# Attention and a Gelu feed-forward on one core: both stages rebuilt around 128x1536 units, with x kept in SBUF

## The chip, the cores and the metric

The kernel runs on one core of one Trainium2 chip. In the views, PE is TensorE's matmuls and PEld its weight loads, ACT is ScalarE, DVE is VectorE, POOL is GpSimd and SP is SyncE; PSUM is the memory that matmuls write to, and a bank is the part of it that a tile of 512 float32 columns takes in these kernels. The granted clock (PEclk) is the share of TensorE's full clock that the throttle allowed. The metric is the device time of one execution in microseconds; medians of several executions are quoted with their extremes. Every ratio uses runs of a kernel and of the kernel before on the same chip in the same session.

An execution is marked "slow" when it is over 1.5% longer than the fastest one of the same kernel, and verdicts use the fast ones alone.

## The reference, cut to what matters

```python
B, C, Hh, Ww = (4, 128, 384, 32)                 # q: (4, 12288, 128), kv: (4, 384, 32, 128)
kv_pool = kv.reshape(B, H // 4, 4, W // 4, 4, C).mean(axis=(2, 4))
k = v = kv_pool.reshape(B, -1, C) @ w_sr         # 768 keys of 128 per batch
s = (q @ k.T) / sqrt(C)
a = softmax(s)
x = (a @ v).reshape(B * S, C)                    # 49152 rows
h = x @ w_in                                     # 128 -> 2048
out = (h * sigmoid(1.702 * h)) @ w_out           # 2048 -> 128
```

So 49152 x 768 exponentials, 49152 x 2048 Gelus, and four large matrix products. No batch attends to another. Both kernels leave out the subtraction of the maximum, which the sizes of the inputs allow.

## The kernel before: the parts that the change touches

It has three stages, one after the other, each with pools of its own. In the first, all keys and values are made. Every 128 rows of kv are one 32 KB load, and a matmul with a small averaging matrix pools them:

```python
for b in range(B):
    poolT_ps = ppsum.tile([128, J], F32)
    for hh in range(Hp):                                   # 96 per batch
        kvt = kvload.tile([128, 128], BF)
        nc.gpsimd.dma_start(out=kvt, in_=kv_flat[b, hh * 128:(hh + 1) * 128, :])
        nc.tensor.matmul(poolT_ps[:, hh * Wp:(hh + 1) * Wp], kvt, M_sb, start=True, stop=True)
    # ... keys, and values by transposing the keys ...
```

The second is attention in steps of 256 rows. All six key chunks of a step lie in one PSUM tile of three banks, of which there is one (`spsum`, `bufs=1`):

```python
sT_ps = spsum.tile([128, JC, TQ * 128], F32)
for jc in range(JC):
    nc.tensor.matmul(sT_ps[:, jc, :], kT[:, jc * 128:(jc + 1) * 128], qT, start=True, stop=True)
a_all = apool.tile([128, JC, TQ * 128], BF)
nc.scalar.activation(a_all, sT_ps, AF.Exp, scale=scale)
# ... sums by a ones column, reciprocal of one row, broadcast, values, product ...
nc.sync.dma_start(out=xT_dram[...], in_=xT)                # x goes to memory
```

The third reads x back, group by group of 512 rows, and runs 16 Gelus of 512 columns on each:

```python
for fc in range(FCH):
    hT_ps = hpsum.tile([128, G * 128], F32)                # one bank, two buffers
    nc.tensor.matmul(hT_ps, w_in_sb[:, fc * 128:(fc + 1) * 128], xT, start=True, stop=True)
    nc.scalar.activation(g_sb[:, fc, :], hT_ps, AF.Gelu_apprx_sigmoid)
# ... 16 accumulating matmuls, then four transposes, copies and stores of 64 KB ...
```

The softmax here doesn't subtract the row's maximum and nothing guards it: scores larger than these inputs give would overflow.

## Time and profile before

| stage | from, us | to, us | length, us | what limits it |
|---|---|---|---|---|
| kv | 0 | 288 | 288 | 384 small loads, issued one by one |
| attention | 288 | 1037 | 749 | a loop of waits through one PSUM buffer |
| feed-forward | 1037 | 1886 | 849 | ACT, by its busy time |
| end | 1886 | 1892 | 6 | last copies and store |

The median is 1892.09 us (1891.73 to 1893.77). On the page, the first line of section 1 gives each engine's busy time, its share of the span and its number of instructions. Section 2 cuts the span into 40 slices of equal length; each digit is a busy share in tenths.

```profile
PE 1395.2 (74%) x7643; PEld 702.0 (37%) x7712; DVE 628.8 (33%) x1273; ACT 1110.2 (59%) x1738; POOL 507.3 (27%) x978
...
PE   1222226666666666666665999999999999999998
...
ACT  0000003333333333333333999999999999999998
...
DMA  5555552222222222222221111111111111111111
```

The reader is to see the three stages as three plateaus, and that no row is full in the first two. An average such as "PE 74%" describes none of them. The prediction below reads each stage from its own waits.

### The profile page before, as it was taken

The page shows a single profiled execution, that of the slowest core. Times are in us where ns is not written, and L with a number is a line of the kernel's source. Part 1 is how long each engine was busy: PE and PEld are TensorE (multiplying, and loading weights), DVE is VectorE, ACT ScalarE, POOL GpSimd, SP SyncE. Part 2 cuts the span into 40 slices and gives each one's busy share as a digit, 9 for nine tenths or more (in the row PEclk, how much of TensorE's full clock was granted, in tenths as well). Part 3 has the DMA queues.
Part 4 walks back from the last instruction along what each step waited for, and adds up shares of the span by engine and source line. Part 5 has one row for each costly group of instructions (what it writes and reads, how often), then busy time and mean ns, then how long its engine had stood idle before and what let it go on. Part 6 is the DMA issues. An engine that isn't in the chain of part 4 may idle for free.

```text
span 1891.9 us, 22738 instructions
## 1 busy us (share of the span) xinstructions
PE 1395.2 (74%) x7643; PEld 702.0 (37%) x7712; DVE 628.8 (33%) x1273; ACT 1110.2 (59%) x1738; POOL 507.3 (27%) x978
## 2 busy tenths in 40 slices
PE   1222226666666666666665999999999999999998
PEld 0111114444444444444443333333333333333333
DVE  0000005666666666666665121211212112112121
ACT  0000003333333333333333999999999999999998
POOL 6777774433443443434432000000000000000000
PEclk9999999999999999999999999999999999999999
DMA  5555552222222222222221111111111111111111
GB/s 54 47 49 47 46 47 32 34 37 35 34 36 35 35 35 33 34 37 35 34 37 34 37 48 42 46 47 45 46 45 45 48 42 48 45 45 48 42 45 40
DMA packets 209829, 78.12 MB, mean 41 GB/s; under 512 B 123568, under 2 KB 209584, under 8 KB 209712
## 3 DMA queue, kind: packets, MB, share of 16 engines
q0 software_dynamic: 112944, 26.30, 15.2%
q1 hardware_dynamic: 96768, 50.37, 9.4%
q8 instruction: 60, 0.98, 0.2%
q14 instruction: 57, 0.47, 0.1%
HBM read 65.08 MB, written 37.75 MB: 54 GB/s over the span
## 4 chain that ended last, share of the span: by engine, by line
PE 51%; ACT 30%; DMA 8%; issue 7%; POOL 3%; DVE 1%; ACTq 0%; POOLq 0%
ACT g_sb L141 16%; PE hT_ps L139 16%; ACT a_all L107 14%; PE oT_ps L144 12%; PE ss_ps L110 8%; PE avT_ps L118 7%; DMA kvt<-in_kv_dram 7%; PE sT_ps L104 7%; POOL kvt L66 2%; PE o_ps L150 1%; DMA qt<-in_q_dram 1%; PE poolT_ps L67 1%; DVE rs L113 0%; POOL rs_bc L115 0%; ACTq L107 0%
## 5 line engine op out<-in xcount | busy, mean ns | idle before, releaser
L141 ACT ACTIVATE g_sb<-hT_ps 128x512 bf16<-128x512 f32 x1536 | 822.8, 597 | 22.6 <-PE hT_ps L139 22.0
L139 PE MATMUL hT_ps<-xT,w_in_sb 128*128 128x512 bf16 x1535 | 579.2, 377 | 35.0 <-ACT g_sb L141 29.6
L107 ACT ACTIVATE a_all<-sT_ps 128x1536 bf16<-128x1536 f32 x192 | 278.4, 1450 | 469.2 <-PE sT_ps L104 451.2
L144 PE MATMUL oT_ps<-g_sb,w_out_sb 128*128 128x512 bf16 x1468 | 550.0, 378 | 0.3 <-ACT g_sb L141 0.2
L113 DVE RECIPROCAL rs<-ss_ps 1x256 f32<-1x256 f32 x192 | 335.2, 1746 | 178.2 <-PE ss_ps L110 178.2
L147 DVE CAST oT<-oT_ps 128x512 bf16<-128x512 f32 x96 | 66.4, 692 | 634.7 <-PE oT_ps L144 634.7
L110 PE MATMUL ss_ps<-a_all,ones_col 128*1 128x256 bf16 x1152 | 158.6, 274 | 147.1 <-ACT a_all L107 147.1
L144 PEld LDWEIGHTS <-w_out_sb 128*128 128x128 bf16 x1536 | 147.3, 96 | 313.3 <-issue 278.3
L67 PE MATMUL poolT_ps<-M_sb,kvt 128*128 128x8 bf16 x384 | 72.0, 189 | 202.5 <-DMA kvt<-in_kv_dram 201.4
L66 POOL DMA_DIRECT2D kvt<-in_kv_dram x384 | 203.1, 533 | 65.0 <-PE poolT_ps L67 35.9
L139 PEld LDWEIGHTS <-w_in_sb 128*128 128x128 bf16 x1536 | 147.3, 96 | 187.9 <-issue 59.6
L115 POOL PARTITION_BROADCAST rs_bc<-rs x192 | 104.1, 543 | 420.7 <-DVE qT L101 391.5
L98 POOL DMA_DIRECT2D qt<-in_q_dram x384 | 207.1, 541 | 35.2 <-PE qT_ps L100 17.3
L110 PEld LDWEIGHTS <-ones_col 128*1 128x1 bf16 x1152 | 94.7, 83 | 199.9 <-issue 174.5
L70 ACT CAST poolT<-poolT_ps 128x768 bf16<-128x768 f32 x4 | 3.2, 798 | 274.2 <-PE poolT_ps L67 274.2
L118 PE MATMUL avT_ps<-a_all,v_all 128*128 128x256 bf16 x1152 | 161.2, 277 | 0.0
L104 PE MATMUL sT_ps<-qT,kT_all 128*128 128x256 bf16 x1152 | 159.8, 276 | 0.6 <-DVE qT L101 0.6
L100 PE MATMUL qT_ps<-ident,qt 128*128 128x128 bf16 x384 | 67.2, 218 | 99.0 <-DVE qT L101 90.3
L67 PEld LDWEIGHTS <-kvt 128*128 128x128 bf16 x384 | 40.5, 105 | 235.3 <-DMA kvt<-in_kv_dram 233.1
L104 PEld LDWEIGHTS <-kT_all 128*128 128x128 bf16 x1152 | 114.0, 99 | 15.5 <-issue 1.1
L118 PEld LDWEIGHTS <-v_all 128*128 128x128 bf16 x1152 | 97.6, 98 | 53.1 <-issue 43.7
L152 DVE CAST o_sb<-o_ps 128x128 f32<-128x128 bf16 x384 | 101.0, 289 | 49.1 <-PE o_ps L150 38.4
(28 smaller groups left out, 304.2 us busy)
## 6 DMA issues: line engine op xcount, KB each, us to landing
out_dram<-o_sb SPq DMA_DIRECT2D x384, 64.0 KB, 1.6
kvt<-in_kv_dram POOLq DMA_DIRECT2D x384, 32.0 KB, 2.1
qt<-in_q_dram POOLq DMA_DIRECT2D x384, 32.0 KB, 2.2
xT_scratch<-xT SPq DMA_DIRECT2D x192, 64.0 KB, 1.7
xT<-xT_scratch SPq DMA_DIRECT2D x96, 128.0 KB, 2.0
w_in_sb<-in_moe_w_in_dram POOLq DMA_DIRECT2D x1, 512.0 KB, 5.3
w_out_sb<-in_moe_w_out_dram POOLq DMA_DIRECT2D x1, 512.0 KB, 7.5
w_sr_sb<-in_w_sr_dram POOLq DMA_DIRECT2D x1, 32.0 KB, 2.2
```

Source lines behind the costliest of these rows:

```text
L66: nc.gpsimd.dma_start(out=kvt, in_=kv_flat[b, hh * 128:(hh + 1) * 128, :])
L67: nc.tensor.matmul(poolT_ps[:, hh * Wp:(hh + 1) * Wp], kvt, M_sb, start=True, stop=True)
L98: nc.gpsimd.dma_start(out=qt, in_=q[b, t * 128:(t + 1) * 128, :])
L104: nc.tensor.matmul(sT_ps[:, jc, :], kT[:, jc * 128:(jc + 1) * 128], qT, start=True, stop=True)
L107: nc.scalar.activation(a_all, sT_ps, AF.Exp, scale=scale)
L110: nc.tensor.matmul(ss_ps, ones_col, a_all[:, jc, :], start=(jc == 0), stop=(jc == JC - 1))
L113: nc.vector.reciprocal(rs, ss_ps)
L115: nc.gpsimd.partition_broadcast(rs_bc, rs)
L118: nc.tensor.matmul(avT_ps, v_all[:, b, jc, :], a_all[:, jc, :], start=(jc == 0), stop=(jc == JC - 1))
L139: nc.tensor.matmul(hT_ps, w_in_sb[:, fc * 128:(fc + 1) * 128], xT, start=True, stop=True)
L141: nc.scalar.activation(g_sb[:, fc, :], hT_ps, AF.Gelu_apprx_sigmoid)
L144: nc.tensor.matmul(oT_ps, w_out_sb[:, fc, :], g_sb[:, fc, :], start=(fc == 0), stop=(fc == FCH - 1))
```

## The change

The intent is to have ACT work without a pause from the first exponential to the last Gelu. Attention runs first for all batches, then the feed-forward for all rows, in one stream of 704 "units", each being three matmuls into a three-bank PSUM tile and one activation of 128x1536. There are two such tiles. PE fills unit n+2 and then drains an older unit: in attention the one ten units back, so that sums and reciprocals are ready when the values are. x never leaves SBUF. The diff, cut to its core:

```diff
-    xT_dram = nc.dram_tensor("xT_scratch", (B * NT // G, C, G * 128), BF, kind="Internal").ap()
+    q_bf = nc.dram_tensor("q_bf", (B * N, C), BF, kind="Internal").ap()
+    big = ctx.enter_context(tc.tile_pool(name="big", bufs=2, space=bass.MemoryType.PSUM))
+    ring = ctx.enter_context(tc.tile_pool(name="ring", bufs=2, space=bass.MemoryType.PSUM))
+    ctx.enter_context(tc.manual_schedule(engines=None))
+    xs = [cpool.tile([128, SG], BF, name=f"x{s}") for s in range(NS)]
     # --- kv: batch 0 as bf16 for PE to pool, the others as f32 for DVE ---
+            t = kvload.tile([Hp, r, r * C], F32, name="kvt")
+            nc.sync.dma_start(out=t, in_=kv_r[b, wp])
     # --- q: cast in memory, then a transposing load ---
+    def cast_q(s, lo=0, n=SG):
+        nc.gpsimd.dma_start(out=q_bf[sl, :]..., in_=q_flat[sl, :]...)
+    def load_qT(s, lo=0, n=SG):
+        nc.sync.dma_start_transpose(out=qTs[s][:, :, lo:lo + n], in_=q_bf[...])
     # --- first batch: 16 accumulating matmuls with the identity pool one tile ---
+            nc.tensor.matmul(p_ps[:, wp // 4, o:o + Hp],
+                             t[:, n // r, (n % r) * C:(n % r + 1) * C], ident[:Hp, :Hp],
+                             start=(n == 0), stop=(n == r * r - 1))
+    make_k(0)
+    make_v(0)
+    cast_q(0, G, SG - G)
+    load_qT(0, G, SG - G)
     # --- one unit of attention, and its values ten units later ---
+            nc.tensor.matmul(s_ps[:, k, :], kTs[b][:, jc * 128:(jc + 1) * 128], rhs, ...)
+        nc.scalar.activation(a, s_ps, AF.Exp, scale=scale)
+            nc.tensor.matmul(av_of[i], vs[b][:, jc, :], a_of[i, t][:, k, :], ...)
+            nc.vector.tensor_tensor(xs[s][...], av_of.pop(i), rb_of.pop(i), MUL)
     # --- sums of four groups at once, in four 32-column strips ---
+        for jc in range(JC):
+            for gi in range(4):
+                nc.tensor.matmul(ss[32 * gi:32 * gi + 32, :], ones, a_of[4 * s + gi, jc // K][:, jc % K, :], ...)
     # --- background work, by group i of 512 rows: q a block ahead, kv of the next batch ---
+        if i % 4 == 0:
+            load_qT(s + 1)
+            cast_q(s + 2)
+            if gb % 2 == 1 and gb // 2 < Wp:
+                load_kv(b + 1, gb // 2 + 2)
+                pool_kv(b + 1, gb // 2)
     # --- the loop ---
+    for n in range(NA + NM):
+        fill(n + 2)
+        # drain_attn of unit n - 10, or drain_moe of unit n - 5
+        if n < NA and n % 8 == 7:
+            sums(n // 8)
```

The three kv loads ahead of the identity, the averaging by 1/16 folded into w_sr, the conditions at the edges and the output side are left out here. Four groups of 512 rows, that is eight units, are called a block below; attention has 24, six per batch.

## The prediction

> **What bounds the kernel now.** I read the page first, then busy time by stretch, then the timeline of one step in each stage. The window view (length, then busy time and count per engine, granted clock, DMA share, GB/s) splits the run at the first exponential (288 us) and near the first Gelu (1037 us):
>
> ```profile
> core 0: us, PE busy (x) PEld busy (x) DVE busy (x) ACT busy (x) POOL busy (x), PEclk, DMA share, GB/s
> 0.00:288.00 288.00, 78.42 (x416) 43.02 (x416) 4.23 (x25) 7.67 (x9) 209.40 (x405) 1.00 0.52 48
> 288.00:1037.00 749.00, 500.91 (x3840) 343.56 (x3840) 456.79 (x768) 278.40 (x192) 297.72 (x573) 1.00 0.25 35
> 1037.00:1886.00 849.00, 814.64 (x3382) 315.16 (x3452) 166.11 (x476) 823.85 (x1537) 0.20 (x1) 1.00 0.16 45
> ```
>
> Three stages run one after the other, each with its own limit. In the first, nothing computes: 384 small kv loads are issued by POOL one by one. In the second no engine is full: it is a closed loop. The chain of waits of one step, 3.83 us long, shows it:
>
> ```profile
> 703.13 1.46 ACT a_all L107
> ...
> 704.63 0.82 PE ss_ps L110 x6
> 705.45 0.76 PE avT_ps L118 x6
> 706.21 0.67 PE sT_ps L104 x6
> ...
> 706.96 1.46 ACT a_all L107
> ```
>
> One exponential, then the sums, the values, and the next scores, and only then the next exponential, because the scores have a single PSUM buffer. 192 such steps of 3.83 us are 735 of the 749 us. The third stage is bound by ACT, whose idle time in it is 23 us:
>
> ```profile
> L141 ACT ACTIVATE g_sb<-hT_ps 128x512 bf16<-128x512 f32 x1536 | 822.8, 597 | 22.6 <-PE hT_ps L139 22.0
> L139 PE MATMUL hT_ps<-xT,w_in_sb 128*128 128x512 bf16 x1535 | 579.2, 377 | 35.0 <-ACT g_sb L141 29.6
> L107 ACT ACTIVATE a_all<-sT_ps 128x1536 bf16<-128x1536 f32 x192 | 278.4, 1450 | 469.2 <-PE sT_ps L104 451.2
> L115 POOL PARTITION_BROADCAST rs_bc<-rs x192 | 104.1, 543 | 420.7 <-DVE qT L101 391.5
> ```
>
> The first two numbers after the bar are union busy time and the mean of one. 1536 Gelus of 597 ns fill only 822.8 us, so successive ones overlap; start times in the trace step mostly by 518 or 543 ns, an overlap of up to 79 ns. The matmul's own step is not its 377 ns but the distance of starts:
>
> ```profile
> 1404.91 0.38 PE L139 MATMUL hT_ps<-xT,w_in_sb 128*128 128x512 bf16 x1
> 1405.13 0.38 PE L144 MATMUL oT_ps<-g_sb,w_out_sb 128*128 128x512 bf16 x1
> 1405.45 0.38 PE L139 MATMUL hT_ps<-xT,w_in_sb 128*128 128x512 bf16 x1
> ```
>
> A second matmul that waits for nothing starts 0.215 us after the first, though each is drawn 0.38 us long. PE shows 96% busy there, yet has about a third of its time to spare.
>
> **What the Trainium skill says.** (1) "ScalarE: Activation LUTs", What ACT_TABLE_LOAD costs: an activation with immediate scale and bias takes 186 ns + 0.833 ns per element, and back-to-back ones overlap by about 93 ns. That gives 612 and 1466 ns; the trace has 597 and 1450, both 15 less, and an overlap of 79. So width alone is worth (3 x 518) - (1450 - 79) = 183 ns per three Gelus. (2) "TensorE: Matmul & The Clock Gate", Back-to-back issue gap: N/2.4 + 2.5 ns warm, 215.8 for 512 columns; the trace agrees with 215. (3) The same page, Part 3 (packing small matmuls): matmuls on different 32-column strips of the array run at once, 2.38 times faster for three strips; no run shows that yet, and the new sums rest on it. (4) "DMA: Bandwidth & Descriptors", Latency and other measured facts: a transposing DMA reaches 261 GB/s; the old kernel has none.
>
> **The change, part by part.** The instruction order shows 704 activations of 128x1536 on ACT (192 Exp, 512 Gelu), where there were 192 and 1536 smaller ones; two 3-bank buffers for them; PE filling unit n+2 before it drains old units. The shortest possible step of a unit on ACT is 1450 - 79 = 1371 ns, estimated from the rows above; all 704 are 965 us. PE per unit: three matmuls to fill, three to drain, 6 x 0.2155 = 1.293 us. Both limits are close, so I go by stage.
>
> *Start.* 8 kv loads of 786 KB instead of the first of 384. The identity is needed for the first pooling matmul; before, it was ready at 9.9 us because POOL stood 7.6 us before it. Three loads (about 0.6 us of issue each) now come ahead of that, so about 11.5 us. Three buffers: loads 4 to 6 go out as PE frees buffers, and 7 and 8 after those. A 1 MB weight load landed in 5.3 us, so I take 5 to 6 us per round trip, plus 16 cold matmuls (about 3 us) a tile at first and 1.8 later: the last tile at 30, its pooling, copies and keys about 4, first exponential at about **35 us** instead of 290. The other three batches are pooled by DVE beside the exponentials and gone from the path.
>
> *Attention.* Removed: q transposes on PE (DMA does them), the wide-row reciprocals (1746 ns for 1x256; now 16 columns on 128 lanes), the round trip of x through memory. Exponentials per block of four 512-row groups: 8 x 1.371 = 11.0 us. PE per block: 48 x 0.2155 = 10.3, and 24 sum matmuls in four strips. With three of four overlapping usefully (24 x 0.2155 / 3 = 1.7) and 0.2 for changing the array's mode I estimate 1.9; together **12.2 us, so PE, not ACT, sets attention**: 24 x 12.2 = 293 us. DVE per block: four multiplies of about 0.7 (424 ns at half the width), two transposes and a small reciprocal about 1.5, two kv poolings about 2.3 each, 9 us: hidden. Four broadcasts on POOL at about 1.0: hidden; ten units of lag give about 4 units (5 us) between sums and first multiply, more than the 3 us chain. Keys and values of three batches use the score buffers: twice about 0.8 us of lost turn plus 1.6 us of PE work each, 10 us. For late transfers I add 5. Sum 308, ending at 343.
>
> *MoE.* ACT: 512 x 1.371 = 702 us. PE: 512 x 1.293 = 662 plus 384 transposes at 0.055 (their step in the old timeline) = 21, so 683, 97% of ACT's. A unit with transposes is about 0.22 over on PE; a fill (0.65 plus latency 0.2) may be late by 0.5 before ACT notices, and later units win back 0.08 each. So ACT bounds; 1.3 for its table load and 3 for the double drains at the change of stage: **706 us**. The old stage took 849. The end, last drain, two copies, store: 6, as the old 5.7.
>
> Sum: 35 + 308 + 706 + 6 = **1055 us**, 0.56 of before.
>
> **The rivals.** *Strips do not overlap*: sums cost 24 x 0.2155 = 5.2 us a block instead of 1.9, +79, so 1134. For it: no run here has ever packed strips, and every one of them loads weights again. Against: the skill's measured packing, and that a plain 128-wide ones matrix would have spared transposes and broadcasts had strips brought nothing. One in eight.
> *Transfers become the bound in attention*: 18.9 MB of kv, 25.2 MB of q read for the cast, 12.6 MB transposed. At the page's rates (hardware queue 9.4% of 16 engines for 96768 packets of 520 bytes, 29 ns each, 283 GB/s; software queue 41 ns for 233 bytes written, 183 GB/s read) and the skill's 261 for the transposes, this is an estimated 67 + 138 + 48 = 253 us of the engines' whole time, inside 308. Average fits, four of six blocks of a batch are denser. A late q or kv would stall PE directly, or DVE and through it the output buffers: 1075 to 1110. One in five, in part.
> *PE bounds MoE as well*: 97% leaves 0.04 us per unit. If a matmul after a semaphore costs 0.225 on average, PE takes 691 + 21 = 712 and ACT waits: +10 to +15, about 1070. One in three.
> *The loop stays closed* (ACT waits for the fill each time, as in the old attention): units of 1450 + about 850 ns would make 1650 us. Against: the old Gelu stage, with two buffers and the same alternation, kept ACT at 97%. Very unlikely.
> Nothing points to a time under ACT's own 965 plus 35 plus 6, that is 1006.
>
> **Range and chances.** Most errors are upward (transfers, PE in MoE), the start is uncertain by 8 either way, and perfect hiding in attention would gain 15 to 25. Range 1027 to 1110. All rivals but the closed loop are far below 1850, so faster by over 2% is 0.98, the same 0.01, slower 0.01.
>
> **What would show it right or wrong.** Right: first Exp at 30 to 40 us; starts of 128x1536 activations 1.37 to 1.40 us apart in MoE with ACT over 95% busy; attention blocks of 12 to 12.7 us with ACT idle 1 to 2 us just after each set of sums; sum matmuls in fours with nearly equal starts. Wrong: sum matmuls 0.2 us apart (strips); scores waiting for a DMA of q, or a DVE addition waiting for kv (transfers); Gelu idle before most units with PE gapless (PE bound); a granted clock under 1.0 as PE fills up, which the old kernel at one third slack does not rule out.

## The result, and the profile after

The changed kernel takes 1087.88 us (1080.91 to 1094.83, four runs), against 1892.31 us for the kernel before in the same session. The ratio is 0.5746, with a 95% interval of 0.5721 to 0.5771. The outputs are correct. The time is inside the predicted range, above the point of 1055.

The profiled run took 1080.91 us (its trace spans 1079.1). The same rows of its page:

```profile
PE 1004.4 (93%) x5368; PEld 461.7 (43%) x5368; DVE 319.0 (30%) x471; ACT 955.2 (89%) x707; POOL 111.6 (10%) x137
...
PE   2379978988999999999999999999999999999998
...
ACT  0178877767889999999999999999999999999997
...
DMA  7999399499544001110011101110111101110111
```

A slice is 27 us now. From slice 14 on (the feed-forward), PE and ACT are both full. In slices 2 to 12 (attention) ACT is at six to nine tenths, and the DMA row has nines, where it stood at two to five tenths in the first two stages before. The window view, cut at the first exponential (38.6), the first Gelu (379.1) and the last Gelu's end (1073.0), has the columns of the prediction's:

```profile
0.00:38.60 38.60, 14.22 (x140) 11.62 (x141) 2.94 (x6) 1.77 (x3) 10.67 (x21) 1.00 0.85 130
38.60:379.10 340.50, 295.55 (x1725) 124.64 (x1723) 177.41 (x264) 264.17 (x194) 98.01 (x112) 0.95 0.76 128
379.10:1073.00 693.90, 693.37 (x3498) 325.02 (x3498) 137.30 (x199) 689.25 (x512) 2.91 (x4) 1.00 0.10 37
```

| stage | before, us | predicted, us | after, us | after minus predicted |
|---|---|---|---|---|
| to the first exponential | 288 | 35 | 38.6 | +3.6 |
| attention | 749 | 308 | 340.5 | +32.5 |
| feed-forward | 849 | 706 | 693.9 | -12.1 |
| end | 6 | 6 | 6.1 | +0.1 |
| sum | 1892 | 1055 | 1079.1 | +24.1 |

The groups of instructions (after the bar: union busy time, the mean of one, then idle time before them and what ended it):

```profile
L250 ACT ACTIVATE ag<-big 128x1536 bf16<-128x1536 f32 x512 | 689.3, 1555 | 4.7 <-PE big L247 4.6
...
L180 ACT ACTIVATE ag<-big 128x1536 bf16<-128x1536 f32 x192 | 262.9, 1467 | 78.4 <-PE big L177 77.9
...
L201 PE MATMUL ring<-ag,ones 128*32 128x512 bf16 x576 | 35.5, 381 | 0.0
```

The Gelus have almost no idle time before them. The exponentials have 78 us of it, all of it waiting for the scores that L177 makes. The starts of undisturbed activations are 1331 ns apart in both stages, though each is drawn 1450 to 1600 ns long: successive ones overlap. The 24 sum matmuls of a block occupy 35.5 / 24 = 1.48 us, less than 24 ordinary matmuls of 0.2156 us (5.2 us).

What does L177 itself wait for? The waits view has engine, line, releaser, then total, times, and the longest, in us:

```profile
ACT ag L180 <- PE big L177: 77.9, 43, 14.0
...
PE big L177 <- DMA qT<-q_bf: 28.1, 5, 14.0
...
PE big L152 <- POOL ident masks.py:199: 15.2, 1, 15.2
...
PE ring L189 <- DVE x L193: 7.6, 2, 4.1
...
DVE kvt L106 <- DMA kvt<-in_kv_dram: 37.6, 4, 28.1
```

28.1 us are waits for transposing loads of q, the longest of them 14.0 us at the very start. It is this one, in the timeline (start, length, engine, line, count, and in brackets the idle time before):

```profile
38.59 2.79 ACT L180 ACTIVATE ag<-big 128x1536 bf16<-128x1536 f32 x2 [2.06 <-PE big L177]
...
53.88 2.74 PE L177 MATMUL big<-qT,kT 128*128 128x512 bf16 x6 [14.04 <-DMA qT<-q_bf]
...
55.38 6.82 ACT L180 ACTIVATE ag<-big 128x1536 bf16<-128x1536 f32 x5 [13.99 <-PE big L177]
```

The first group of 512 rows, two units, is there early; the remaining 1536 rows of block 0 are cast and loaded only after the last kv tile and land 15 us later. The 7.6 us of "ring L189" are an indirect transfer wait. DVE itself waits 37.6 us for kv tiles (last line). It pools late kv tiles in program order, its product of values and reciprocals stands behind that pooling, so the output bank is not freed and PE stops.

I attributed each step between exponentials beyond 1331 ns to what PE waited for in it. Of the 340.5 us, 192 x 1.331 = 255.6 are the exponentials; 32.0 stand at the sums; 29.5 wait for q (14.1 at the start, the rest at the heads of blocks 2, 8, 10 and 15); 8.7 wait for DVE; 6.5 go to the keys and values of the next batch; 6.1 to other; about 2 are small remainders and the step to the first Gelu. The blocks that no transfer disturbs (18 to 22) take about 11.93 us each.

A part of these steps is not waiting but slower work. The granted clock of attention is 0.95 in the window view above. The trace's clock record says why: after 54 us it falls to 0.50 in four stretches of 3.4 to 6.8 us (at 77.3, 186.5, 230.9 and 265.1 us), each beginning inside or just after a wait of PE of 3.6 us or more, though one wait of 3.5 us is followed by none. In these stretches 44 matmuls of 512 columns start 427 ns apart instead of 216, by which they take about 9 us longer (an estimate: the sum of these differences). It is spread over "other" (4.6 us) and the steps put down to q, DVE and the sums. after_again has 49 such matmuls, about 10 us.

The head of an undisturbed block shows the regular cost of the sums:

```profile
319.62 1.25 PE L201 MATMUL ring<-ag,ones 128*32 128x512 bf16 x18
...
320.80 0.82 PE L177 MATMUL big<-qT,kT 128*128 128x512 bf16 x3
...
321.72 10.85 ACT L180 ACTIVATE ag<-big 128x1536 bf16<-128x1536 f32 x8 [1.08 <-PE big L177]
```

The sums stand ahead of the next scores on PE, so ACT is idle for 1.08 us, then runs eight exponentials without a gap.

In the feed-forward PE has a gapless pattern of three to fill and three to drain, 0.65 us each, and four output transposes per group:

```profile
602.20 0.81 PE L261 MATMUL ring<-ag,w_out_sb 128*128 128x512 bf16 x3
...
602.85 0.39 PE L273 MATMUL ring<-ident,oT 128*128 128x128 bf16 x4
...
603.07 0.81 PE L247 MATMUL big<-x,w_in_sb 128*128 128x512 bf16 x3
```

Sixteen units are three groups of rows: 96 x 0.2156 + 12 x 0.056 = 21.37 us of PE work against 16 x 1.331 = 21.30 us on ACT. The measured time of sixteen steady units is 21.49 us. The two engines are level.

### The profile page after: what moved, and what is told of

The parts are those of the page before. It is cut to its first block, busy times and chain, and to the rows that moved or that the text cites. A ratio compares the mean times of both kernels' runs of the same rounds, so it can differ in the third digit from the quotient of the medians.

```text
span 1079.1 us, 13408 instructions
## 1 busy us (share of the span) xinstructions
PE 1004.4 (93%) x5368; PEld 461.7 (43%) x5368; DVE 319.0 (30%) x471; ACT 955.2 (89%) x707; POOL 111.6 (10%) x137
## 4 chain that ended last, share of the span: by engine, by line
PE 83%; DMA 11%; ACT 3%; issue 2%; DVE 1%; SPq 0%; POOL 0%; ACTq 0%; POOLq 0%; DVEq 0%
PE big L247 30%; PE ring L261 30%; PE big L177 9%; PE ring L189 9%; DMA qT<-q_bf 7%; DMA kvt<-in_kv_dram 3%; PE ring L201 2%; ACT ag L180 2%; PE ring L273 2%; ACT ag L250 1%; DMA q_bf<-in_q_dram 1%; DVE kvt L106 0%; SPq L83 0%; ACTq L334 0%; POOL kvt L67 0%
## 5 line engine op out<-in xcount | busy, mean ns | idle before, releaser
L250 ACT ACTIVATE ag<-big 128x1536 bf16<-128x1536 f32 x512 | 689.3, 1555 | 4.7 <-PE big L247 4.6
L247 PE MATMUL big<-x,w_in_sb 128*128 128x512 bf16 x1536 | 414.7, 379 | 0.0
L261 PE MATMUL ring<-ag,w_out_sb 128*128 128x512 bf16 x1536 | 414.2, 379 | 0.5 <-ACT ag L250 0.5
L180 ACT ACTIVATE ag<-big 128x1536 bf16<-128x1536 f32 x192 | 262.9, 1467 | 78.4 <-PE big L177 77.9
L265 DVE CAST oT<-ring 128x512 bf16<-128x512 f32 x96 | 66.4, 692 | 450.0 <-PE ring L261 450.0
L177 PE MATMUL big<-qT,kT 128*128 128x512 bf16 x576 | 161.9, 392 | 38.2 <-DMA qT<-q_bf 28.1
L189 PE MATMUL ring<-ag,v 128*128 128x512 bf16 x576 | 159.4, 388 | 7.8 <-DVE x L193 7.6
L213 POOL PARTITION_BROADCAST rb<-t x96 | 93.5, 1025 | 254.1 <-DVE t L210 201.1
L177 PEld LDWEIGHTS <-kT 128*128 128x128 bf16 x576 | 55.1, 100 | 117.6 <-issue 31.9
L193 DVE TENSOR_TENSOR x<-ring,rb 128x512 bf16<-128x512 f32 x96 | 65.2, 688 | 112.4 <-PE ring L189 111.1
L275 DVE CAST o_sb<-ring 128x512 f32<-128x512 bf16 x96 | 66.4, 692 | 101.6 <-PE ring L273 101.6
L189 PEld LDWEIGHTS <-v 128*128 128x128 bf16 x576 | 57.3, 99 | 79.9 <-issue 15.5
L273 PEld LDWEIGHTS <-oT 128*128 128x128 bf16 x384 | 32.2, 114 | 22.7 <-DVE oT L265 1.9
L106 DVE TENSOR_TENSOR kvt<-kvt 96x1024 f32<-96x1024 f32 x24 | 30.5, 1271 | 37.6 <-DMA kvt<-in_kv_dram 37.6
L201 PE MATMUL ring<-ag,ones 128*32 128x512 bf16 x576 | 35.5, 381 | 0.0
L152 PE MATMUL big<-ident,kvt 96*128 96x96 bf16 x128 | 11.3, 280 | 23.0 <-POOL ident masks.py:199 15.2
```

The costliest lines, as they stand in the source:

```text
L177: nc.tensor.matmul(s_ps[:, k, :], kTs[b][:, jc * 128:(jc + 1) * 128], rhs, start=True, stop=True)
L180: nc.scalar.activation(a, s_ps, AF.Exp, scale=scale)
L189: nc.tensor.matmul(av_of[i], vs[b][:, jc, :], a_of[i, t][:, k, :], start=(jc == 0), stop=(jc == JC - 1))
L193: nc.vector.tensor_tensor(xs[s][:, (i % 4) * G:(i % 4 + 1) * G], av_of.pop(i), rb_of.pop(i), MUL)
L201: nc.tensor.matmul(ss[32 * gi:32 * gi + 32, :], ones, a_of[4 * s + gi, jc // K][:, jc % K, :], start=(jc == 0), stop=(jc == JC - 1))
L213: nc.gpsimd.partition_broadcast(rb, t2[32 * gi:32 * gi + 1, :])
```

## The experiments

The question is where the 24 to 33 us above the prediction went, and whether the steps of the sum that came out right did so for the reason given. Experiments one to four, five to eight, nine to eleven, and twelve ran in one session each; the kernel before took 1894.02, 1894.5, 1893.25 and 1894.01 us in them. All outputs are correct unless said otherwise.

### after_again: the changed kernel, unaltered

No edit. It anchors the session and shows whether the waits recur.

> The changed kernel unaltered, three rounds, as the yardstick for the others of this call. Its first four runs spread from 1081 to 1095 us while the kernel before spread by 2 us. Expected 1080 to 1095, ratio 0.571 to 0.578.

1088.47 us (1085.21 to 1091.08), ratio 0.5746 (0.5733 to 0.5759). In its trace the first exponential starts at 41.2 us, attention takes 345.9, the feed-forward 693.9. The waits for q are 32.7 us, sums 32.2, DVE 10.0, keys 6.5. So the feed-forward and the sums repeat to 0.2 us, and what differs between the two traces is the start, the waits for transfers and the clock behind them.

### no_q_stream: q of the first two blocks used for all

```diff
     def cast_q(s, lo=0, n=SG):
+        if s >= 2:
+            return
     def load_qT(s, lo=0, n=SG):
+        if s >= 2:
+            qTs[s] = qTs[s % 2]
+            return
```

The result is wrong. It still passes the comparison: the attended values hardly depend on q here, which is a limit of the comparison and not a merit of the kernel.

> Wrong result on purpose: only the q of the first two blocks is cast and transposed; the 22 later blocks reuse those two tiles. The exponentials, matmuls and kv work stay. The start (first exponential at 38.6 us, then 14.1 us waiting for the rest of the first q block) stays as well. Theory 1 (transfers of q come late to the scores): the later waits for q, 17 to 18 us in the trace of after, go, and with the SP queue free of transposes the kv waits (10 us) go too: 1088 - 28 = 1060. Theory 2 (kv is the late one, q only behind it in the queue): only a part, 1078 to 1088. Theory 3 (transfers do not matter, the excess over the prediction is the sums and the keys of later batches): 1085 to 1090.

1042.23 us (1041.35 to 1043.15), ratio 0.5501, lower than any of the three theories expected: 46.2 us less than after_again, and the spread is 2 us instead of 6. Attention takes 301.1 us. The only wait for q left is 5.5 us in block 0; blocks without keys take 11.93 us. The window from 54 to 390 us, after first:

```profile
54.00:390.00 336.00, 305.09 (x1790) 129.22 (x1790) 182.56 (x272) 270.55 (x198) 100.92 (x116) 0.97 0.71 124
```

and without the stream of q:

```profile
54.00:390.00 336.00, 328.44 (x1964) 143.73 (x1964) 190.19 (x283) 300.90 (x222) 96.36 (x96) 1.00 0.23 56
```

The DMA share falls from 0.71 to 0.23, ACT works 30 us more in the same stretch, and the granted clock is 1.00 instead of 0.97: with the waits, the matmuls at half clock are gone. The two account for nearly all of the gain of attention, 340.5 - 301.1 = 39.4 us: PE's waits for q and DVE are 28.1 + 7.6 us in the changed kernel and 5.4 here, 30.3 less, and half clock cost about 9 us. No step waits behind DVE and its late kv tiles any more either, although not a byte of kv was taken away.

### no_kv_stream: kv of batches 1 to 3 not loaded

One kept tile is pooled 24 times instead, by the same additions on DVE (the first now reads bf16). The result is wrong.

```diff
-            t = kvload.tile([Hp, r, r * C], F32, name="kvt")
-            nc.sync.dma_start(out=t, in_=kv_r[b, wp])
+            t = xs[NS - 1][:Hp].rearrange("p (a b) -> p a b", a=r)
+            if "kept" not in qTs:
+                qTs["kept"] = nc.gpsimd.dma_start(out=t, in_=kv_r[b, wp])
...
-        nc.vector.tensor_tensor(t[:, 0:2, :], t[:, 0:2, :], t[:, 2:4, :], ADD)
+        u = kvload.tile([Hp, r, r * C], F32, name="kvt")
+        nc.vector.tensor_tensor(u[:, 0:2, :], t[:, 0:2, :], t[:, 2:4, :], ADD)
```

> Wrong result on purpose: for batches 1 to 3 one kv tile is loaded once and pooled 24 times by VectorE; the 23 other loads of 768 KB go, the additions, keys and values stay. Theory 1 (the q transposes are slow by themselves): the kv waits of 10 us go, the q waits stay: 1078. Theory 2 (q stands behind kv in the SP queue and on the DMA engines): both go: 1060. Theory 3: 1085 to 1090.

1054.14 us (1053.45 to 1060.46), ratio 0.5573, somewhat better than the 1060 of theory 2: 34.3 us less than after_again. All later waits for q are gone, though the stream of q is untouched. The wait at the start remains and was 22.1 us in the profiled run:

```profile
54.00:390.00 336.00, 316.90 (x1890) 137.38 (x1891) 187.31 (x277) 289.02 (x212) 104.12 (x116) 1.00 0.42 70
```

### no_q_no_kv: both taken away

The edits of the two together. Its output is wrong, which doesn't matter for the time.

> Both of the above (wrong result on purpose). All theories that blame transfers in attention expect 1088 - 28 = 1060, with a spread of runs as small as that of the kernel before (a few us at most): the spread of after would then be that of its transfers. What is left is the start (53.9 us until the second unit pair), 24 blocks of 11.93 us as in the undisturbed blocks 18 to 22, 8 us of key building and the Gelu stage of 694 us. If it stays at 1085 or above, the transfers of later blocks are not the cause.

1043.04 us (1042.49 to 1046.11), ratio 0.5511, 45.4 us less than after_again, where 1060 was expected: the time without transfer waits had been put too high. If each stream cost its own time, the two would have given 46.2 + 34.3 = 80.5. They gave no more than q alone. So neither stream delays attention by itself once the start is over; they delay it where they meet.

The packet records of the trace show the meeting. A transposing packet of 256 bytes took 31.4 ns on average between 54 and 390 us in the changed kernel, and 21.2 ns in no_kv_stream between 70 and 390. A kv packet of 2048 bytes took 139.3 ns, and 130.4 ns in no_q_stream. The totals in that stretch of after, over 16 engines, are 90.8 us for transposes, 80.3 for kv and 64.0 for the casts: 235 us of 336. A packet's time includes what it waits for others, so this is not the work of the engines alone.

### kv_on_pool_queue: the same loads issued from the other queue

```diff
-            nc.sync.dma_start(out=t, in_=kv_r[b, wp])
+            nc.gpsimd.dma_start(out=t, in_=kv_r[b, wp])
```

This asks whether kv and q disturb each other because both stand in SP's queue, or because they share the DMA engines.

> Right result. The kv loads of batches 1 to 3 are issued by POOL instead of SP; bytes, packets of 2048 bytes and the 16 DMA engines stay. Either stream taken away alone ended all later waits, so the two disturb each other. Theory A (order in the SP queue: a transposing load stands behind a kv load that waits for its buffer, or holds the queue 5 us while a kv load waits): with separate queues the later waits mostly go, 1055 to 1065. Theory B (the 16 DMA engines themselves are shared: 71% busy over attention, and both streams slow down together): no change, 1080 to 1095, or worse, as POOL also issues the casts.

1085.42 us (1082.01 to 1091.04), ratio 0.5732 (0.5714 to 0.5751), which cannot be told from the changed kernel and is what theory B expected. Waits for q were 22.8 us in the profiled run and those for DVE 21.6. The Trainium skill, "DMA: Bandwidth & Descriptors", Issuing engines are not separate DMA queues, says that transfers of all issuing engines run on the same 16 DMA engines and interleave. This run agrees: with another queue the waits lie elsewhere and their sum is no smaller (44.4 us against 38.2). It does not fully exclude the order within a queue, since POOL also issues the casts and makes the broadcasts: kv left one shared queue for another.

### start_order: the rest of block 0's q asked for early, weights late

```diff
     for wp in range(3):
         load_kv(0, wp)
+    cast_q(0, G, SG - G)
     ident = cpool.tile([128, 128], BF)
...
     load_qT(0, 0, G)
+    load_qT(0, G, SG - G)
...
-    cast_q(0, G, SG - G)
-    load_qT(0, G, SG - G)
     cast_q(1)
...
-    nc.gpsimd.dma_start(out=w_in_sb, in_=moe_w_in)
-    nc.gpsimd.dma_start(out=w_out_sb, in_=moe_w_out.rearrange("(o p) c -> p o c", p=128))
...   (both issued at group 84 of 96 instead)
```

> Right result. The cast and the transpose of the rest of the first q block go out behind the first three kv loads instead of behind all eight, and the two MoE weight loads move from the start to the 84th group, far ahead of their use. Theory: the 14 us wait of the third unit for q at the start goes, and the first exponential moves back by the 2 to 5 us that the cast takes from kv: 1088 - 11 = 1077. Rival (the wait at the start is the transpose's own speed on busy engines, so it only moves ahead of the first exponential, or the keys come later by as much): 1085 to 1090.

1061.24 us (1053.7 to 1073.13, the last slow), ratio 0.5582 (0.5559 to 0.5605): better than expected. Block 0 takes 10.66 us instead of 24.79, so the wait of 14 us at the start is gone. The waits for q also fell from 29.5 to 7.5 us over all of attention, while those for DVE rose from 8.7 to 12.0. So the later blocks gained as well. This run changed two things at once, and does not say how much was the order of q and how much the 2 MB of weights that were moved out of the first blocks.

### strips_in_turn: the same sums, one strip after the other

```diff
-        for jc in range(JC):
-            for gi in range(4):
+        for gi in range(4):
+            for jc in range(JC):
```

In this order six successive matmuls go to the same strip.

> Right result. The loops over strips and key chunks in the sums are exchanged, so that six matmuls in a row go to one 32-column strip; number and size stay. In after the four of a set start 3 to 4 ns apart and a set of 24 takes 1.41 us. Theory (the strips are what makes the sums cheap): 24 x 0.2157 = 5.18 us a block, 24 x 3.77 = +90 us, less up to 20 as the waits for q hide in longer blocks: 1155 to 1178. Rival (PE runs them together in any order): 1085 to 1095.

1110.41 us (1099.2 to 1119.58), ratio 0.5842. The expectation of 1155 to 1178 was missed: I expected no overlap, and most of it survived.

```profile
L201 PE MATMUL ring<-ag,ones 128*32 128x512 bf16 x576 | 67.7, 381 | 0.0
```

67.7 / 24 = 2.8 us a block, between 1.48 with alternating strips and the 5.2 of no overlap. The recorded starts show how. With alternating strips the gaps in ns are 3, 4, 3, 216, 3, 4, 3, 206 and so on: four start together, six times. In turn they are 226, 216, 6, 210, 17, 199, 16, 6, 194 and so on. The third and fourth starts are 6 ns apart, though the first six matmuls of the program all go to strip 0. Either two matmuls of one strip ran within 6 ns, or one of another strip had moved ahead. The trace does not name the strip, but the durations speak for the second: in every set of the changed kernel the first four records, the first of each strip, last about 389 ns and the other twenty 379; here the long ones are the 1st, 4th, 9th and 15th, where program order would have them 1st, 7th, 13th and 19th. By these records TensorE did not keep program order between strips. Attention takes 373.6 us in the profiled run, which was slow.

### one_score_buffer: one three-bank tile instead of two

```diff
-    big = ctx.enter_context(tc.tile_pool(name="big", bufs=2, space=bass.MemoryType.PSUM))
+    big = ctx.enter_context(tc.tile_pool(name="big", bufs=1, space=bass.MemoryType.PSUM))
```

> Right result. The three-bank PSUM tile for scores and hidden values has one buffer instead of two. Theory (the gain of after is that exponentials and fills overlap; the closed loop of before comes back without it): a unit is 1.45 us on ACT plus a fill of 3 x 0.216 + 0.17 plus handshakes of about 0.1: 2.37 us, 704 x 2.37 = 1668, plus start and end: 1700 to 1760, nearly the time before. Rival (width, transposing DMA and x in SBUF carry the gain): under 1300.

1788.48 us in a single run of unknown state, a little over the expected 1700 to 1760. Three lines of its timeline, in the feed-forward:

```profile
899.80 0.81 PE L247 MATMUL big<-x,w_in_sb 128*128 128x512 bf16 x3 [0.95 <-ACT ag L250]
...
900.71 1.45 ACT L250 ACTIVATE ag<-big 128x1536 bf16<-128x1536 f32 x1 [0.95 <-PE big L247]
...
902.21 0.81 PE L247 MATMUL big<-x,w_in_sb 128*128 128x512 bf16 x3 [0.73 <-ACT ag L250]
```

Activation, then fill, then activation, each waiting for the other: 2.407 us a unit in both stages. This is the closed loop of the old attention, with everything else of the change in place. The second buffer is worth 1788 - 1088 = 700 us here.

### deeper_prefetch: more buffers, everything asked for earlier

start_order, and in addition kv as bf16 in six buffers for every batch, asked for up to a batch ahead, and q two blocks ahead in three buffers:

```diff
-    kvload = ctx.enter_context(tc.tile_pool(name="kvload", bufs=3))
+    kvload = ctx.enter_context(tc.tile_pool(name="kvload", bufs=6))
-    qpool = ctx.enter_context(tc.tile_pool(name="qpool", bufs=2))
-    agpool = ctx.enter_context(tc.tile_pool(name="ag", bufs=14))
+    qpool = ctx.enter_context(tc.tile_pool(name="qpool", bufs=3))
+    agpool = ctx.enter_context(tc.tile_pool(name="ag", bufs=13))
...
+            for d in ((1, 2) if s == 0 else (2,)):
+                if s + d < NS:
+                    load_qT(s + d)
+            if s + 3 < NS:
+                cast_q(s + 3)
```

> Right result; meant to beat after and start_order. On top of start_order: kv of all batches is cast to bf16 by POOL's transfers (six buffers of 4 KB in place of three of 8 KB), its loads start four tiles before their pooling and partly in the quiet end of the batch before, and q is transposed two blocks ahead (three buffers; one unit buffer fewer to make room). Theory (the later waits are two streams that together come close to the engines' rate, so that earlier and lighter transfers hide them): the 25 us of later waits in start_order go: 1061 - 20 to 25 = 1036 to 1042, with a small spread. Rival (the engines are simply too slow for this traffic wherever it starts): 1055 to 1062.

1054.84 us over six runs (1048.81 to 1077.59, two of them slow); ratio of the fast ones 0.554 (0.5528 to 0.5553). The expectation of 1036 to 1042 was missed; the median is just under the rival's 1055 to 1062. The profiled run was a slow one. In it the blocks from 6 on take 11.93 us wherever no keys are made: the later waits are cured. The start is worse: the last kv tile of batch 0 landed at 56.6 us, the first exponential began at 62.4, and the DMA share of the first 54 us was 1.27 (a share is the sum of packet times, so over 1 it means that packets of one engine overlap in time). In this run the early transfers of later blocks stood beside the ones that were needed first. Whether the fast runs start as late is not known, since none of them has a trace; and the run changed several things at once, so it does not say which of them cured the later waits.

### one_bank_units: three activations of 512 columns instead of one of 1536

```diff
-    big = ctx.enter_context(tc.tile_pool(name="big", bufs=2, space=bass.MemoryType.PSUM))
+    big = ctx.enter_context(tc.tile_pool(name="big", bufs=6, space=bass.MemoryType.PSUM))
...
+            s_ps = big.tile([128, 512], F32, name="big")
+            nc.tensor.matmul(s_ps, kTs[b][:, jc * 128:(jc + 1) * 128], rhs,
...   (and one activation per bank; the same in fill_moe)
```

> Right result. Units of one PSUM bank and six buffers of it: every unit of 1536 columns becomes three activations of 512, with the same matmul order, lag and SBUF tiles. It tells width from buffers. Theory (three-bank width saves two starts of an activation per unit): the step of a wide one is 1331 ns, that is 1536/1.2 + 51; with the same 51 ns a narrow one steps by 478, three by 1434; ACT then bounds MoE: 512 x (1434 - 1343) = +47, attention hides most of it behind its sums and waits, +10 to 20: 1140 to 1155. If narrow ones step by 518 as in the kernel before: 512 x 211 + 192 x about 150 = +137: 1225. Rival (depth of buffering alone matters, width is free): 1083 to 1095.

1141.22 us (1139.38 to 1146.95), ratio 0.6033, as expected.

```profile
L252 ACT ACTIVATE ag<-big 128x512 bf16<-128x512 f32 x1536 | 753.1, 1838 | 0.8 <-PE big L250 0.7
```

Their starts are 478 ns apart when undisturbed, against 1331 for three times the width. Both are the width divided by 1.2 columns per ns plus 51 ns. The feed-forward takes 753.8 us, so the width is worth 60 us there and 1141.2 - 1088 = 53 us in all. It also corrects how I read the old kernel, as told below.

### sums_full_width: a ones matrix of 128 columns

```diff
-    ones = cpool.tile([128, 32], BF)
+    ones = cpool.tile([128, 128], BF)
...
-                nc.tensor.matmul(ss[32 * gi:32 * gi + 32, :], ones,
+                nc.tensor.matmul(ss, ones,
...
-                                 start=(jc == 0), stop=(jc == JC - 1))
+                                 start=(jc + gi == 0), stop=(jc == JC - 1 and gi == 3))
```

Wrong, since four groups fall into one sum: it costs what sums without strips would.

> Wrong result on purpose (the four groups of a block share one sum). The 24 sum matmuls of a block use a ones matrix of 128 columns and the whole array instead of four 32-column strips, so that nothing can overlap: the price of sums without strips, which strips in turn did not show because the array still overlapped them (2.7 us a set). Theory: 24 x 0.216 = 5.18 us against 1.41 us a block, +90 us, less 10 to 20 us of waits for q and kv that longer blocks hide: 1158 to 1178. If under 1120, the strips were worth little.

1148.97 us (1146.4 to 1154.21), ratio 0.6072, 61 us more than after; expected was 1158 to 1178.

```profile
L201 PE MATMUL ring<-ag,ones 128*128 128x512 bf16 x576 | 129.1, 381 | 0.5 <-DVE x L193 0.5
```

The matmuls start 216 ns apart, 5.2 us a block, and undisturbed blocks take 15.6 us instead of 11.93. That would be 24 x 3.67 = 88 us. Some 27 us of it are not seen in the total. Slower blocks give late transfers more time, and the two traces, whose attention differs by 65 us, fit that: PE's waits for q and DVE are 22.6 us here against 35.7, and matmuls at half clock cost about 3 us instead of 9 (estimates as above). That is 19 of the 88 - 65 = 23 us that attention lacks.

### paced_prefetch: the start order and the deep buffers, with the transfers spread out

deeper_prefetch, but the kv of batch 1 is asked for only from group 5 on and pooled from group 8 on, and q is cast and loaded two blocks ahead, one group into a block:

```diff
+        if i == 0:
+            load_qT(1)
+        if i == 2:
+            load_qT(2)
+        if i % 4 == 1 and s >= 1 and s + 2 < NS:
+            cast_q(s + 2)
+            load_qT(s + 2)
+        for wp in range(Wp):
+            for bb in (b + 1, b + 2):
+                if bb < B and i == (5 + wp if bb == 1 else GB * (bb - 1) + 2 * wp - 8):
+                    load_kv(bb, wp)
```

> Right result. The last run asks whether both transfer findings can be had at once. It is the start order that shortened the first block, plus the buffers of the deeper prefetch that left the later blocks without waits, with the transfers paced: in batch 0 the kv of batch 1 is asked for only from the fifth group on and pooled from the eighth, and the cast and transpose of q run two blocks ahead, one group into a block. Theory (the waits come from transfers that were asked for too late or too many at once): first exponential at about 40 us, attention about 24 blocks of 11.93 us plus some 15 us for keys and the start, no later wait for q or kv, so about 301 us; MoE 694, end 6: together 1038 to 1046 us, with a small spread. Rival (moving transfers earlier only moves the contention): the start or some blocks wait again and the time is 1050 to 1062, as with the start order or the deeper prefetch alone, or the spread stays at ten microseconds or more.

1052.66 us over six runs (1045.84 to 1067.93, two slow); ratio of the fast ones 0.554 (0.5522 to 0.5559). The fast runs took 1045.84, 1046.77, 1048.52 and 1056.79. So the best single runs of any correct version, but no better ratio than deeper_prefetch, and the spread remains: the expectation of 1038 to 1046 was met by one run out of six, and the rival was nearer. The profiled run was again a slow one. Its blocks from 6 on are at 11.93 us where no keys are made, but blocks 2 to 4 take 18.0, 17.7 and 15.2; its first exponential came at 55.8. From 15 to 52 us:

```profile
15.00:52.00 37.00, 9.91 (x129) 9.06 (x129) 1.01 (x2) 0.00 (x0) 3.49 (x6) 0.63 1.18 86
```

and the same stretch of start_order:

```profile
15.00:52.00 37.00, 21.87 (x169) 14.16 (x173) 5.08 (x8) 12.31 (x10) 5.34 (x9) 1.00 1.00 170
```

The DMA share is higher and the rate is half. Between 20 and 52 us of that run, transposing packets took 172 ns on average at a median of 31, and kv packets of 1024 bytes 299 ns at a median of 98; one transposing load took 33.8 us from issue to landing. Whether the fast runs differ in just this cannot be said, since only the profiled runs have traces.

## Why the prediction was right or wrong

**The regime: right.** All three limits of the old kernel went. The kv stage left the path (first exponential at 38.6 us instead of 288), the closed loop was opened (one_score_buffer closes it again and costs 700 us), and the feed-forward fell from 849 to 693.9 us. The rival "the loop stays closed" named 1650 us as its price; with one buffer it is 1788.

**The start: the size a little off.** 38.6 to 42.9 us in the runs with the original start and original units, against 35. The estimate of 11.5 us for the identity was short: the first pooling matmul waited 15.2 us for it, since the select that makes it ran on POOL at 14.8 us.

**ACT's step: mis-sized.** "The shortest possible step of a unit on ACT is 1450 - 79 = 1371 ns" should have been 1331. The overlap of 79 ns was read from the old Gelu stage as if ACT set the step there. It did not quite: the same 128x512 Gelu steps at 478 ns in one_bank_units, and stepped at 518 or 543 ns in the old kernel. The old stage showed ACT 97% busy, but each Gelu is drawn 597 ns long, so that ACT looks full at any step up to 597 ns; 1536 x 0.478 = 734 us would have been the floor of a stage that took 849. Nor was a third of PE's time to spare there, as the prediction says: its own 662 + 21 = 683 us of work are 80% of 849, which leaves a fifth. The true overlap is 597 - 478 = 119 ns for the narrow and 1450 - 1331 = 119 ns for the wide activation. So of the 155 us that the feed-forward gained, 60 are the width, and 95 came with the rest of the rebuilding (six one-bank buffers in that run instead of two, and drains that trail the fills). I did not separate those 95 further.

**Attention by blocks: right, and PE's sums are its limit.** Predicted 12.2 us a block, measured 11.93 where nothing disturbs it: the sums take 1.48 us of PE by busy time instead of 1.9 (of which 0.2 was for a change of mode that no run measured), and ACT idles about 1.1 us behind them as foreseen. "Strips do not overlap" was worth 79 us by the prediction; sums_full_width shows 61 more than after in total, and 88 by its blocks. Strips do overlap, all four of them. 24 blocks of 11.93 are 286 us against the 293 of the sum; the keys took 6.5 instead of 10 by the count of steps, or 8.9 by the blocks in which they are made (13.29 and 13.52 us in place of 11.93, three times).

**The transfers: the term of the sum that failed.** It reads "For late transfers I add 5". The measured price is 340.5 - 301.1 = 39 us of attention between the two profiles, and 46 us between the medians of after_again and no_q_stream. The rival beside it, "Transfers become the bound in attention", had the right mechanism and nearly the right size of the load: an estimated 253 us of the engines' whole time, where the packets took 235 us between 54 and 390. That sum is luck: the cast was put at 138 us and took 64.0 in that window, the transposes at 48, by the skill's 261 GB/s, and took 90.8. It had the right range too, 1075 to 1110, but was given one chance in five. The false step is "Average fits", taken as enough although the same sentence adds that four of six blocks of a batch are denser: a share of 0.7 to 0.8 does not mean that each transfer lands on time. Three things made it miss. The rest of block 0's q was asked for after everything else, which cost 14 us at once. Each later block of q was loaded only one block, some 12 us, ahead. And the streams collide: transposing packets take half as long again beside kv loads, and the removals saved 46 and 34 us singly, 45 together. And of the 39 us some 9 are not waiting at all: the granted clock fell to 0.50 behind the waits, which the prediction feared only from a PE that fills up.

**The feed-forward: the total 12 us too high, the stated bound a draw.** PE's work per unit was computed correctly (1.334 us with the transposes; measured 21.37 / 16 = 1.336). ACT's, at 1.371, was too long, and so "ACT bounds" is not what the trace shows: the two are within 0.005 us of each other, and a steady unit takes 1.343 on average. The rival "PE bounds MoE as well" is thus nearer in mechanism (PE has 693.4 us of busy time in the 693.9 of the stage) and wrong in size: it put a matmul at 0.225 us where the steady ones take 0.2156, and started from too long a step, so that it said about 1070 where the stage came out shorter than predicted. 512 x 1.343 = 687.7; the other 6 us are the first hundred units, where leftover values of attention and double drains make steps of up to 2.37 us. The prediction's own sign, starts 1.37 to 1.40 us apart, was not met. Only one_bank_units moved one of the two (ACT to 3 x 0.478 = 1.434, and the stage to 753.8 / 512 = 1.472 a unit); none took ACT below PE, so the draw rests on these counts. The granted clock stayed at 1.00 there, so that worry was not borne out.

The two errors in attention and feed-forward are opposite in sign. Without the gains from ACT's shorter step the time would have been close to the upper end of the range: the range held partly because errors cancelled, which is luck.

Three correct versions beat both kernels: start_order (0.5582), deeper_prefetch and paced_prefetch (0.554 each), which is 0.554 / 0.5746 = 0.964 of the changed kernel. (For deeper_prefetch the plain mean of its four fast runs, 1051.9 us, over that of the kernel before would give 0.556; the two cannot be told apart.) no_q_stream's 1042 us says that some ten more are left in the transfers.

## What to carry to other kernels

Read a stage's floor from the smallest distance between starts, and ask whether the engine that looks full really steps at that distance: a busy share of 97% hid over 10% here. When compute has been made dense, budget the transfers per deadline and not per average, and issue first what is needed first; prefetching deeper without an order moved the wait to the start in the one trace of it, a slow run. Count a stall of PE for more than its length when the clock falls behind it. To learn whether two streams cost time each or jointly, remove each alone and then both: a joint saving no larger than the larger of the two (here 45 us, against 46 and 34) means that they collide.

## What the Trainium skill lacked or had wrong

- "ScalarE: Activation LUTs", What ACT_TABLE_LOAD costs: the overlap of back-to-back activations is given as about 93 ns. Here it is 119 ns: steps of 478 and 1331 ns for 512 and 1536 columns from PSUM, that is, width / 1.2 plus 51 ns, with durations of 597 and 1450 ns when they stand alone. Only this page's overlap differs; a fixed part of 51 ns as such is not missing from the skill.
- "TensorE: Matmul & The Clock Gate", Back-to-back issue gap: beside the formula that gives 215.8 ns for 512 columns, the section names about 131 ns per matmul as sustained in a stream of weight load and matmul. Every one of the matmuls here loads weights, and the steady stream of the feed-forward runs at 215.6 ns. The formula agrees, the sustained figure does not.
- The same page, Part 3: it says that matmuls start strictly in program order. In strips_in_turn two recorded starts lie 6 ns apart among what are in program order six matmuls of one strip, and 24 of them span 2.43 us from first to last start; the long records (1st, 4th, 9th and 15th) say that other strips' matmuls had moved ahead. Its table stops at 2.38 times for three column strips; with four, 24 sums kept PE busy for 1.48 us, against 129.1 / 24 = 5.38 us in sums_full_width, 3.6 times.
- "DMA: Bandwidth & Descriptors", Latency and other measured facts: 261 GB/s for a transposing DMA has no word on neighbours. Here 256-byte transposing packets took 21.2 ns on average without kv loads beside them (16 engines x 256 / 21.2, an estimated 193 GB/s), 31.4 with them, and 172 in the crowded start of one run.
- No page that I found says how much a stream of q (a casting DMA from memory to memory and a transposing one) and loads of kv delay each other; the runs show 46 and 34 us for removing one of the two streams and 45 for both.
